# A linear-attention, mixture and gated-product kernel: whole-line values, denominators gathered in one transfer, conversions spread, weights split on another engine, and a re-planned order

## The chip, the core and the metric

The program runs on one NeuronCore of a Trainium2 chip. Its engines are TensorE (PE, whose weight loads the profile calls PEld), VectorE (DVE), ScalarE (ACT), GpSimd (POOL) and SyncE (SP), which here issues every transfer. The metric is the device time of one execution in microseconds (us); of several runs the median counts.

## What is computed

Three parts follow each other, all in fp32 (three of the late weights arrive as float64):

```python
def phi(x):
    proj = np.einsum('bhsd,df->bhsf', x, w_phi)
    proj = proj - np.max(np.abs(proj), axis=-1, keepdims=True)
    return np.concatenate([np.exp(proj), np.exp(-proj)], axis=-1)
q_p, k_p = (phi(q), phi(k))
kv = np.einsum('bhsf,bhsd->bhfd', k_p, v)
z = np.sum(k_p, axis=2)
num = np.einsum('bhsf,bhfd->bhsd', q_p, kv)
den = np.einsum('bhsf,bhf->bhs', q_p, z)[..., None] + 1e-06
x = num / den                                   # 4 x 8 heads, 576 tokens, 64 wide -> x: 2304 x 512
p = probs / (probs.sum(-1, keepdims=True) + 1e-09)
x = sum(p[:, e:e+1] * (np.maximum(x @ w1[e], 0) @ w2[e]) for e in range(4))   # 512 -> 1024 -> 512
out = ((x @ v1) * (x @ v2) @ w3) @ w_out        # 512 -> 1024 -> 1024 -> 512
```

## The kernel before

**Attention** goes by 16 pairs of heads. For pair p, `k_side` loads the keys (`kr`) and values (`vx`), projects the keys, subtracts the largest magnitude, takes both exponentials and sums them against the values (tile `kvp`, matmuls of line 498). The value tile holds, for each of five token tiles and two heads, 64 values and two columns of ones, which give the sum z; before the change the ones are set once by POOL and a load fills only the 64 columns. Pairs in `KSPLIT` do the key projection with each operand split into a rounded part and a remainder, three passes (`PASSES`); the others use one full-precision product. `q_side` does the same for the queries (`Pq`, `Ps`, `Eq`) and multiplies with `kvp`'s copy (`num`). The result `xq` has 64 rows of numerators and, in the other half, rows that all hold the denominator. One denominator row per head goes to DRAM (`den`), comes back as 128 partitions of 9 (`d9`, which the trace calls d), gets 1e-6 added and is inverted on DVE (lines 602, 605), goes to DRAM again (`rd`) and comes back broadcast over 64 partitions per head (`rb`); DVE multiplies (`xr`, line 615).

**Experts** go by visits: one visit is a quarter of one expert's hidden width, for one or two groups of 768 tokens. The first visits (`plain`) work on group 0 while attention is still running. Later visits use Strassen's seven products (`strassen_up`: banks upa, upb, upc; ACT copies a bank out as `s`, line 764; DVE adds them, line 771; `relu` makes the two parts of `h`; `expert_down` multiplies with w2, tile dn, and DVE adds to `acc`, line 833). Each weight is loaded as `raw` and split: ACT casts (line 290), then DVE or POOL subtracts (line 292); for Strassen POOL also forms sums (`sm`, line 326). Then come visits that `fold` w3 and w_out into one matrix (tile psw), taken in turn with experts, and last the gated products (`gates`), whose result `g` is split by ACT and DVE.

**Conversions.** The float64 weights become fp32 on the chip, in 40 half matrices (`nearest_tasks`, tile near): a load (line 342), one ACT step into a tile f (line 345), five DVE steps (lines 348, 351, 355, 358, 361), and a write-out of f to DRAM (line 364). There is one tile f, so the next ACT step waits for the write-out before it. `run_visits` puts these steps among the expert work. A visit's turn with one group starts a number of them: two in the turn of group 1, one in the other, 20 in the visits for groups 1 and 0, and 20 in those for groups 1 and 2.

**The order** on each engine is written out by a planner, `Prog.run`: it plays all operations with a duration for each (`ns`), a delay after a result (`TAIL`) and after a transfer (`wait`), and a priority, and emits them in the order in which they start there. `AHEAD` and `KLEAD` set the priority of each pair against the expert turns. Each engine then takes its list in order, and SyncE its transfers too.

The planner's delays and the pace of the conversions are in these lines:

```python
SYNC = 45.0
TAIL = {"PE": 175.0, "DVE": 85.0, "ACT": 100.0, "POOL": 85.0}
def dma(fn, nbytes, **kw):
    return op(SP, 500, fn, wait=1600 + nbytes / 180.0, **kw)
for _ in range(0 if len(pairs) < 2 else 1 + (i == 1)):
    if len(near_todo) > (20 if c >= KA else 0):
```

## Time and profile before

| what | value |
|---|---|
| median of 3 runs | 1337.9 us |
| lowest run | 1337.41 us |
| the profiled execution | 1336.39 us |
| its span, first to last instruction | 1334.6 us |
| mean granted PE clock | 0.991 of full speed |
| busy: PE, DVE, ACT, POOL | 1286.8, 972.0, 614.4, 478.3 us |

Busy is the time in which an engine's instructions run, in the profiled execution. A stretch of the span is read by itself: attention alone runs to 94 us, attention with plain visits to 338, the experts for groups 1 and 0 to 602, groups 1 and 2, then group 2, with the fold to 1052, and the gated products to the end. The waits name, for each idle time of an engine, whose signal ended it. The chain is the work that ended last, followed back from the end.

### The profile page before, as it was taken

To read this page: it belongs to the slowest core of one execution; us is meant where nothing else is said; L and a number is where in the kernel's file an instruction comes from. 1 tells how busy PE (TensorE), PEld (TensorE's weight loads), DVE (VectorE), ACT (ScalarE), POOL (GpSimd) and SP (SyncE) were. 2 spreads that over 40 slices of the span, in tenths; PEclk is the share of its full clock that TensorE was granted. 3 is DMA by queue.
4 is the path that set the end of the run, shared out by engine and by line. 5 is a ranking of instruction groups with operands and counts; after the bars stand their busy time and mean duration, and the time that the engine had idled before them with its cause. 6 is when DMAs were issued, how large, how long until landed. Compare 5 with 4: busy or idle time off the path is not lost.

```text
span 1334.6 us, 18054 instructions
## 1 busy us (share of the span) xinstructions
PE 1286.8 (96%) x6739; PEld 1154.1 (86%) x6739; DVE 972.0 (73%) x1513; ACT 614.4 (46%) x1198; POOL 478.3 (36%) x348
## 2 busy tenths in 40 slices
PE   8889999999999899999989999999999999999998
PEld 7778888998887788898878898988888899999897
DVE  6678898877977788877877888766656555476555
ACT  5677875763433233334333333443434454243451
POOL 3333321222432333302333333134465553244671
PEclk8999999999999999999999999999999999999999
DMA  5554443322333332203334333212232211013211
GB/s 146 147 167 110 136 134 114 90 66 58 103 104 102 103 103 95 87 32 111 127 110 151 126 127 111 78 58 80 103 111 97 85 32 34 30 33 110 80 48 48
DMA packets 73032, 126.28 MB, mean 95 GB/s; under 512 B 32720, under 2 KB 37200, under 8 KB 72944
## 3 DMA queue, kind: packets, MB, share of 16 engines
q1 hardware_dynamic: 72944, 125.13, 30.6%
q8 instruction: 53, 0.87, 0.3%
q14 instruction: 35, 0.29, 0.1%
HBM read 107.66 MB, written 17.45 MB: 94 GB/s over the span
## 4 chain that ended last, share of the span: by engine, by line
PE 62%; DVE 16%; DMA 11%; ACT 5%; issue 4%; POOL 1%; SPq 1%; ACTq 0%; POOLq 0%; DVEq 0%
PE dn L810 25%; PE upa L741 8%; PE upb L741 4%; PE kvp L498 3%; PE psw L883 2%; DMA rb<-rd 2%; DVE acc L833 2%; PE num L587 2%; DMA near_v<-near 2%; PE upc L741 2%; PE up L741 2%; DVE near L361 2%; DMA near_wo<-near 2%; DMA rd<-d 1%; PE upa_3b L741 1%
## 5 line engine op out<-in xcount | busy, mean ns | idle before, releaser
L810 PE MATMUL dn<-w_b,h 128*128 128x512 f32 x1728 | 424.9, 393 | 4.9 <-DVE acc L833 3.6
L810 PEld LDWEIGHTS dn<-w_b,h 128*128 128x128 f32 x1728 | 322.3, 189 | 66.5 <-DVE acc L833 5.2
L833 DVE SCALAR_TENSOR_TENSOR acc<-dn,pn,acc 128x512 f32<-128x512 f32 x270 | 198.3, 744 | 56.2 <-PE dn L810 55.3
L741 PE MATMUL upa<-x_T,w_a 128*128 128x384 f32 x720 | 148.7, 341 | 16.2 <-ACT s L764 16.1
L292 POOL TENSOR_TENSOR w_b<-raw_b,w_b 128x1024 fp32r<-128x1024 f32 x32 | 80.2, 2507 | 227.1 <-ACT w_b L290 227.1
L563 POOL PARTITION_ALL_REDUCE M<-Ps x64 | 86.3, 1352 | 200.1 <-ACT Ps L560 157.4
L741 PEld LDWEIGHTS upa<-x_T,w_a 128*128 128x128 f32 x720 | 127.7, 189 | 29.8 <-ACT s L764 24.7
L292 POOL TENSOR_TENSOR w_a<-raw_a,w_a 128x768 fp32r<-128x768 f32 x32 | 61.4, 1917 | 233.7 <-ACT w_a L290 233.6
L290 ACT CAST w_b<-raw_b 128x1024 fp32r<-128x1024 f32 x59 | 62.0, 1051 | 103.3 <-PE dn L810 64.9
L810 PE MATMUL dn<-w_b,g 128*128 128x512 f32 x432 | 104.5, 390 | 0.0
L764 ACT COPY s<-upa 128x384 f32<-128x384 f32 x120 | 57.3, 477 | 101.0 <-PE upa L741 100.7
L326 POOL TENSOR_TENSOR sm_a<-raw_a 128x256 f32<-128x256 f32 x64 | 52.5, 821 | 141.0 <-DMA raw_a<-w 60.6
L810 PEld LDWEIGHTS dn<-w_b,g 128*128 128x128 f32 x432 | 80.6, 188 | 14.2
L292 POOL TENSOR_TENSOR w_a<-sm_a,w_a 128x1024 fp32r<-128x1024 f32 x32 | 80.3, 2511 | 10.6 <-ACT w_a L290 10.6
L498 PEld LDWEIGHTS kvp<-vx,E 128*128 128x128 f32 x576 | 74.4, 202 | 6.4 <-ACT E L490 3.3
L587 PE MATMUL num<-Eq,KV 128*128 128x288 f32 x328 | 71.9, 348 | 6.9 <-ACT Eq L571 2.7
L498 PE MATMUL kvp<-vx,E 128*128 128x66 f32 (+1 forms) x576 | 75.9, 284 | 2.6 <-DMA vx<-vt 1.3
L741 PE MATMUL up<-x_B,w_a 128*128 128x384 f32 x384 | 71.7, 337 | 0.0
L741 PEld LDWEIGHTS up<-x_B,w_a 128*128 128x128 f32 x384 | 66.7, 188 | 0.6
L587 PEld LDWEIGHTS num<-Eq,KV 128*128 128x128 f32 x328 | 51.7, 191 | 15.8 <-ACT Eq L571 3.8
L290 ACT CAST w_a<-raw_a 128x768 fp32r<-128x768 f32 (+2 forms) x59 | 48.3, 818 | 35.7 <-PE upb L741 23.6
L571 ACT ACTIVATE Eq<-Ps 128x288 f32<-128x288 f32 x128 | 50.7, 444 | 22.0 <-DVE Ps L566 20.3
(217 smaller groups left out, 2416.2 us busy)
## 6 DMA issues: line engine op xcount, KB each, us to landing
raw_a<-w SPq DMA_DIRECT2D x35, 512.0 KB
raw_b<-w SPq DMA_DIRECT2D x35, 512.0 KB
qr<-qT SPq DMA_DIRECT2D x32, 288.0 KB
near<-w3T SPq DMA_DIRECT2D x16, 512.0 KB
raw_b<-near_wo SPq DMA_DIRECT2D x16, 512.0 KB
near<-v SPq DMA_DIRECT2D x16, 512.0 KB
vx<-vt SPq DMA_DIRECT2D x16, 320.0 KB
kr<-kT SPq DMA_DIRECT2D x15, 320.0 KB
```

The costliest lines, as they stand in the source:

```text
L290: lambda: op(ACT, act(n), lambda: nc.scalar.copy(out=hi(), in_=raw[1]()), reads=[raw[0]], fills=[w], after=after),
L292: lambda: op(eng, ns, lambda: e.tensor_tensor(out=lo(), in0=raw[1](), in1=hi().bitcast(F32), op=ALU.subtract), reads=[raw[0], w], fills=[w ...
L326: ops.append(lambda k=k, out_=out_, a=a, b=b, how=how: op(eng, ns, lambda: e.tensor_tensor(out=out_(), in0=a(), in1=b(), op=how), reads=[r ...
L361: lambda: op(DVE, dve(n), lambda: v.tensor_tensor(out=f(), in0=f(), in1=t(), op=ALU.add), reads=[t], writes=[f]),
L498: nc.tensor.matmul(kvp()[:, a].rearrange("p h d -> p (h d)") if rest else kvp()[:, a, h], E()[:, a] if rest else E()[:, t, a, h], w()[:, 4 ...
L563: op(POOL, 1171, lambda M=M, Ps=Ps: nc.gpsimd.partition_all_reduce(M(), Ps(), channels=128, reduce_op=bass_isa.ReduceOp.absmax), reads=[Ps ...
L571: op(ACT, act(HS), lambda a=a, E=E, Ps=Ps: nc.scalar.activation(out=E()[:, a], in_=Ps(), func=AF.Exp, scale=1.0 - 2 * a), reads=[Ps], fill ...
L587: nc.tensor.matmul(num(), KV[i]()[:, a, 2 * h:2 * h + 2].rearrange("p c d -> p (c d)"), EE[j]()[:, a], start=n == 0, stop=n == len(parts) - 1)
L741: nc.tensor.matmul(ps(), w()[:, a, i, kk * 128:kk * 128 + 128], x()[:, j, kk], start=first and n == 0, stop=last and n == total - 1, skip_ ...
L764: op(ACT, act(TB, False), lambda: nc.scalar.copy(out=t(), in_=ps()), reads=[ps], writes=[t], after=start["C"])
L810: nc.tensor.matmul(ps(), hs[fc]()[:, x, t * 128:(t + 1) * 128], w()[:, fc * 2:fc * 2 + 2, y], start=fc == 0 and n == 0, stop=fc == 1 and n ...
L833: op(DVE, dve(DM), lambda a=a, ps=ps, share=share: nc.vector.scalar_tensor_tensor(out=a(), in0=ps(), scalar=share(), in1=a(), op0=ALU.mult ...
```

## The change

- The host lays the values out with their columns of ones, so one load fills the whole tile; POOL's fills at the start are gone.
- The denominator row of each head goes straight from `xq` to 64 partitions of `d9`; the trip through `den` in DRAM is gone.
- Pair 13 leaves `KSPLIT`.
- Conversions: one per turn, 16 in the visits for groups 1 and 0, 16 for groups 1 and 2, and 8 in the visits for group 2 alone (`NEAR`, two in the first of these); v1 and v2 are taken by quarters.
- The fold's weights are split with POOL's subtraction in the 8 fold visits for quarters 0 to 7, DVE's after that.
- The gate product is written over its second operand, which lies in PSUM for three of four blocks, so that cast and subtraction read PSUM.
- The planner: 100 ns more after each result, 500 ns more after each transfer (`LATE`) and more for the small ones (`extra`), 6% on DVE and ACT (`MORE`), measured lengths for the conversion steps, other `KLEAD` and `AHEAD`.

```diff
-KSPLIT = (2, 4, 7, 10, 11, 12, 13, 14, 15)
+KSPLIT = (2, 4, 7, 10, 11, 12, 14, 15)
...
-AHEAD = (0.05, 0.53, 0.67, 0.83, 1.78, 1.99, 3.11, 3.51, 7.79, 8.19, 8.47, 9.88)
+AHEAD = (0.05, 0.53, 0.67, 0.83, 1.78, 1.99, 3.11, 4.01, 7.79, 7.93, 8.42, 9.83)
+NEAR = (24, 8, 0)
-BESIDE = 1.3
+BESIDE = 1.5
...
-        self.n, self.eng, self.ns, self.fn, self.prio, self.wait = n, eng, ns, fn, prio, wait
+        self.n, self.eng, self.fn, self.prio = n, eng, fn, prio
+        self.ns = ns * Prog.MORE if eng in ("DVE", "ACT") else ns
+        self.wait = wait + Prog.LATE if eng == "SP" else wait
...
-    TAIL = {"PE": 175.0, "DVE": 85.0, "ACT": 100.0, "POOL": 85.0}
+    TAIL = {"PE": 275.0, "DVE": 185.0, "ACT": 200.0, "POOL": 185.0}
+    LATE, MORE = 500.0, 1.06
...
-            out=w().rearrange("p t h d -> p (t h) d")[:, :, 0:64], in_=vt[b, pr].rearrange("p (c d) -> p c d", d=64)
-        ),
-            327680, writes=[w])
+        dma(lambda: nc.sync.dma_start(out=w().rearrange("p t h d -> p (t h d)"), in_=vt[b, pr]), 337920, writes=[w])
...
             dma(lambda h=h, dr=dr: nc.sync.dma_start(
-                out=den()[:, h * S:(h + 1) * S], in_=xq()[dr:dr + 1, h]
-            ), 2304, reads=[xq], fills=[den])
-        d9 = V("at", [128, 2 * S // 128], F32, "d9", 3, f"d9_{p}")
-        dma(lambda: nc.sync.dma_start(out=d9(), in_=den()[0].rearrange("(p c) -> p c", p=128)), 4608,
-            reads=[den], writes=[d9])
+                out=d9()[h * 64:(h + 1) * 64], in_=xq()[dr:dr + 1, h].rearrange("o (p c) -> o p c", p=64)
+            ), 2304, extra=1500, reads=[xq], fills=[d9])
...
-                lambda: n3().rearrange("p (k q f) -> p k q f", k=2, q=2)[:, :, q % 2], "ring1", f"a{v}", reads=[n3], n=2
+                lambda: n3().rearrange("p (k q f) -> p k q f", k=2, q=2)[:, :, q % 2], "ring1", f"a{v}", reads=[n3], n=2,
+                eng=POOL if c < KA else DVE
             ))
-            made.append(split_tasks(lambda: no(), "ring2", f"b{v}", reads=[no]))
+            made.append(split_tasks(lambda: no(), "ring2", f"b{v}", reads=[no], eng=POOL if c < KA else DVE))
...
-                    for _ in range(0 if len(pairs) < 2 else 1 + (i == 1)):
-                        if len(near_todo) > (20 if c >= KA else 0):
+                    phase = 2 if len(pairs) < 2 else int(c < KA)
+                    for _ in range(2 if phase == 2 and c == KA else 1):
+                        if len(near_todo) > NEAR[phase]:
...
-                        to = gates[ft]
-                        op(DVE, dve(TB), lambda to=to, src=src: nc.vector.tensor_tensor(
-                            out=to(), in0=src(), in1=to(), op=ALU.mult
-                        ), reads=[src], writes=[to])
+                        g = gates[ft]
+                        op(DVE, dve(TB), lambda g=g, src=src: nc.vector.tensor_tensor(
+                            out=src(), in0=src(), in1=g(), op=ALU.mult
+                        ), reads=[g], writes=[src])
...
-    for w in vx:
-        op(POOL, 1000, lambda w=w: nc.gpsimd.memset(w(), 1.0), writes=[w])
...
+    vpad = np.zeros((B, 4, 128, 5, 2, D + 2), v.dtype)
+    vpad[:, :, :, :4, :, D:] = 1
```

SyncE, while pairs 0 to 3 are under way (kr: keys, qr: queries, vx: values, the number behind each name is the pair). Before, from the gathering of pair 0's denominators to its broadcast:

```order
L596 DMA den0_332<-xq0_296 1x576
L534 DMA qr3_0_396<-qT 128x576
L600 DMA d9_0_415<-den0_332 128x9
L596 DMA den1_443<-xq1_406 1x576
L606 DMA rd0_453<-d9_0_415 128x9
L610 DMA rb0_479<-rd0_453 64x576 x2
```

and now:

```order
L600 DMA d9_0_359<-xq0_311 64x1x9
L600 DMA d9_1_463<-xq1_427 64x1x9
L607 DMA rd0_471<-d9_0_359 128x9
L538 DMA qr3_1_479<-qT 128x576
L443 DMA vx0_123<-vt 128x660
L600 DMA d9_1_463<-xq1_427 64x1x9
L611 DMA rb0_535<-rd0_471 64x576 x2
```

The first hop through DRAM is gone, and three other transfers have moved between rd0 and rb0.

ACT, in the visits for groups 1 and 0 (h12_0 and s12_0 are visit 12, group 0; near0 is the conversion's step into tile f). Before, between two conversion steps:

```order
L345 ACTIVATE near0_3831<-near0_3831 128x512
L290 CAST w_b13_4277<-raw_b13_4006 128x4x256
L796 ACTIVATE h12_0_00_4297<-upc12_0_4280 128x384
L764 COPY s2_12_0_4306<-upa12_0_4251 128x384
L764 COPY s3_12_0_4329<-upa12_0_4251 128x384
L796 ACTIVATE h12_0_11_4332<-s3_12_0_4329 128x384
L345 ACTIVATE near0_3831<-near0_3831 128x512
```

and now:

```order
L352 ACTIVATE near0_3799<-near0_3799 128x512
L297 CAST w_b13_4209<-raw_b13_3950 128x4x256
L766 COPY s1_12_0_4219<-upa12_0_4202 128x384
L766 COPY s2_12_0_4249<-upa12_0_4202 128x384
L798 ACTIVATE h12_0_00_4253<-upc12_0_4223 128x384
L766 COPY s3_12_0_4270<-upa12_0_4202 128x384
L798 ACTIVATE h12_0_11_4280<-s3_12_0_4270 128x384
L352 ACTIVATE near0_3799<-near0_3799 128x512
```

The next step stands seven places after the one before it, where it stood six, and group 0's turn now has one of them.

POOL, at visits 21 and 22 (w_a22 and w_b22: the expert's weights; w_a21 and w_b21: the fold's; sm: Strassen's sums). Before:

```order
L326 TENSOR_TENSOR sm_a22_6136<-raw_a22_6051,sm_a22_6136 128x256
L292 TENSOR_TENSOR w_a22_6292<-raw_a22_6051,w_a22_6292 128x3x256
L292 TENSOR_TENSOR w_a22_6292<-sm_a22_6136,w_a22_6292 128x4x256
L292 TENSOR_TENSOR w_b22_6366<-raw_b22_6060,w_b22_6366 128x4x256
L326 TENSOR_TENSOR sm_a24_6435<-raw_a24_6389 128x256
```

and now:

```order
L299 TENSOR_TENSOR w_a21_5950<-raw_a21_5828,w_a21_5950 128x2x256
L333 TENSOR_TENSOR sm_a22_6078<-raw_a22_5983 128x256
L333 TENSOR_TENSOR sm_a22_6078<-sm_a22_6078,raw_a22_5983 128x256
L333 TENSOR_TENSOR sm_a22_6078<-raw_a22_5983 128x256
L333 TENSOR_TENSOR sm_a22_6078<-raw_a22_5983,sm_a22_6078 128x256
L299 TENSOR_TENSOR w_b21_6138<-raw_b21_5902,w_b21_6138 128x4x256
L299 TENSOR_TENSOR w_a22_6206<-raw_a22_5983,w_a22_6206 128x3x256
L299 TENSOR_TENSOR w_a22_6206<-sm_a22_6078,w_a22_6206 128x4x256
L299 TENSOR_TENSOR w_b22_6280<-raw_b22_5994,w_b22_6280 128x4x256
```

The fold's two subtractions have come to stand among those of the expert after it.

## Rows read from the trace of the kernel before

**Rows 1.** Busy time by stretch: length, then busy us of each engine, PEclk, DMA

```profile
0.00:25.00 25.00, 21.64 (x93) 17.09 (x94) 15.37 (x34) 13.06 (x31) 8.31 (x17) 0.80 0.56 147
25.00:225.00 200.00, 185.64 (x1136) 165.60 (x1134) 161.19 (x301) 142.43 (x340) 59.67 (x45) 0.98 0.50 138
...
350.00:450.00 100.00, 91.76 (x436) 80.42 (x436) 80.37 (x118) 33.79 (x60) 41.68 (x30) 0.97 0.33 101
450.00:675.00 225.00, 220.89 (x1098) 196.16 (x1097) 181.96 (x275) 82.91 (x148) 60.41 (x38) 1.00 0.30 94
600.00:875.00 275.00, 266.96 (x1322) 237.05 (x1321) 221.64 (x332) 107.14 (x187) 78.00 (x52) 1.00 0.36 114
675.00:775.00 100.00, 93.07 (x456) 82.05 (x455) 77.01 (x120) 35.17 (x62) 26.08 (x20) 1.00 0.40 126
1075.00:1225.00 150.00, 150.00 (x786) 140.24 (x785) 82.19 (x125) 60.03 (x107) 64.75 (x49) 1.00 0.13 39
1225.00:1275.00 50.00, 48.03 (x246) 43.34 (x245) 32.08 (x47) 22.99 (x39) 29.53 (x23) 1.00 0.32 106
```

**Rows 2.** Waits, whole span: engine, line, releaser, us, times, longest

```profile
DVE xr L615 <- DMA rb<-rd: 16.7, 12, 4.2
PE upa L741 <- ACT s L764: 16.1, 17, 2.2
DVE d L602 <- DMA d<-den: 9.9, 7, 2.6
PE kvp L498 <- DMA vx<-vt: 1.3, 1, 1.3
```

**Rows 3.** Waits of SyncE's queue, whole span

```profile
SPq L600 <- DMA den<-xq: 18.8, 12, 4.8
```

**Rows 4.** Chain that ended last, 25 to 235 us: shares

```profile
by line: DMA rb<-rd 11.8%; DMA rd<-d 8.9%; PE kvp L498 7.3%; DVE xr L615 7.3%; PE num L587 6.2%; DMA d<-den 5.5%; issue 4.5%; DMA vx<-vt 4.4%; DMA den<-xq 3.9%; DVE Ps L566 3.0%; ACT Eq L571 2.9%; DVE w_a L292 2.2%; DMA raw_a<-w 2.1%; DVE E
```

**Rows 5.** Chain that ended last, 350 to 775 us: shares

```profile
by line: PE dn L810 23.6%; PE upa L741 12.6%; issue 6.7%; PE upb L741 5.7%; DMA near_v<-near 5.7%; DVE near L361 4.8%; DMA near_wo<-near 4.8%; DVE acc L833 4.5%; DMA near_w<-near 3.8%; DVE near L358 3.5%; DVE near L351 3.0%; DVE near L355 2
```

**Rows 6.** The conversion tile: ns min/median/max; last who waited for it

```profile
L355 DVE TENSOR_SCALAR near<-near x40: 409/418/2512, 355.5 to 838.8; 128x512 int32<-128x512 int32 x40
...
L361 DVE TENSOR_TENSOR near<-near x40: 674/684/2774, 358.3 to 841.8; 128x512 f32<-128x512 f32 x40
...
  ACT near L345: 50.4, 30
```

**Rows 7.** Chain pieces: key projections, full precision and split

```profile
20.75 0.86 PE P L463 x4
...
267.60 1.43 PE P L463 x12
```

**Rows 8.** Timeline 397 to 409 us: start, us, engine, instruction, idle before

```profile
397.73 2.17 DVE L351 SCALAR_TENSOR_TENSOR near<-near 128x512 int32<-128x512 int32 x1
...
399.30 2.86 POOL L292 TENSOR_TENSOR w_a<-sm_a,w_a 128x1024 fp32r<-128x1024 f32 x1
...
400.29 2.14 DVE L355 TENSOR_SCALAR near<-near 128x512 int32<-128x512 int32 x1
...
408.17 1.70 PE L741 MATMUL upa<-x_T,w_a 128*128 128x384 f32 x6 [2.23 <-ACT s L764]
```

**Rows 9.** Groups by shape: weight splits: count, busy us, mean ns

```profile
L292 POOL TENSOR_TENSOR w_b<-raw_b,w_b 128x1024 fp32r<-128x1024 f32 x32 | 80.2, 2507 | 227.1 <-ACT w_b L290 227.1
...
L292 DVE TENSOR_TENSOR w_b<-raw_b,w_b 128x1024 fp32r<-128x1024 f32 x27 | 37.0, 1371 | 3.3 <-ACT w_b L290 2.6 <-issue 0.4
L292 DVE TENSOR_TENSOR w_a<-raw_a,w_a 128x512 fp32r<-128x512 f32 x16 | 30.3, 1896 | 8.6 <-ACT w_a L290 8.6
```

**Rows 10.** The gate tile g: ns min/median/max

```profile
L292 DVE TENSOR_TENSOR g<-s_3a,g x12: 548/551/559, 1065.0 to 1201.7; 128x384 fp32r<-128x384 f32 x12
...
L292 DVE TENSOR_TENSOR g<-s_4a,g x12: 643/1653/2551, 1081.0 to 1226.3; 128x384 fp32r<-128x384 f32 x12
```

More of the change, by code (lines that the diff above doesn't have):

```diff
@@ L284, in beside, with split_ops @@
         return dve(n) * (BESIDE if "C" in start else 1)
-    def split_ops(raw, hi, lo, n, w, eng, after=()):
-        e, ns = (nc.gpsimd, gp(n)) if eng == POOL else (nc.vector, beside(n))
+    def split_ops(raw, hi, lo, n, w, eng, after=(), sbuf=True):
+        e, ns = (nc.gpsimd, gp(n)) if eng == POOL else (nc.vector, beside(n) if sbuf else dve(n))
         return [
-            lambda: op(ACT, act(n), lambda: nc.scalar.copy(out=hi(), in_=raw[1]()), reads=[raw[0]], fills=[w],
+            lambda: op(ACT, act(n, sbuf), lambda: nc.scalar.copy(out=hi(), in_=raw[1]()), reads=[raw[0]], fills=[w],
                        after=after),
@@ L504, in total @@
                             )
-            op(PE, 2 * mm4(132) if rest else nt * 4 * 210, total, reads=[E, w], writes=[kvp])
+            op(PE, 2 * mm4(132) if rest else nt * 4 * 224, total, reads=[E, w], writes=[kvp])
         for g, (t0, nt) in enumerate(KG0 if not p else KG):
@@ L797, in relu @@
            reads=[src], fills=[h])
-        op(DVE, dve(TB), lambda: nc.vector.scalar_tensor_tensor(
+        op(DVE, beside(TB) if sbuf else dve(TB), lambda: nc.vector.scalar_tensor_tensor(
             out=h()[:, 1], in0=src(), scalar=0.0, in1=h()[:, 0].bitcast(F32), op0=ALU.max, op1=ALU.subtract,
@@ L899, in run_visits @@
         turn, behind = 0, []
-        near_todo = deque((k, i, h) for k, n in (("wo", 4), ("w3", 8), ("v1", 4), ("v2", 4)) for i in range(n) for h in range(2))
+        near_todo = deque(
+            (k, i, h) for k, n in (("wo", range(4)), ("w3", range(8)), *((x, (c,)) for c in range(4) for x in ("v1", "v2")))
+            for i in n for h in range(2)
+        )
         srcs = {"wo": w_out, "w3": w3T, "v1": v1, "v2": v2}
@@ L903, in run_visits @@
         drain()
-        rooms, later = [None, None], []
+        rooms, later = {}, []
         for v, (kind, c, pairs, blocks) in enumerate(visits):
@@ L990, in fused_kernel @@
     qr0 = load_q(0, 0)
-    for w in vx:
-        op(POOL, 1000, lambda w=w: nc.gpsimd.memset(w(), 1.0), writes=[w])
-        for h in range(2):
-            op(POOL, 100, lambda w=w, h=h: nc.gpsimd.memset(w()[64 - 64 * h:128 - 64 * h, 4, h], 0.0), writes=[w])
     op(POOL, 1000, lambda: make_identity(nc, eye()), writes=[eye])
```

42 lines of the change are left out of this document (20 added, 22 removed).

## The prediction, on record before the kernel ran

> **What bounds the kernel now.** I read the busy time by stretch first, because the shares over the whole span hide that this program is two programs. TensorE (PE) is the engine everything else feeds: from 1075 to 1225 us it is busy 150.00 of 150 us, so nothing but its own work sets the time there [rows 1]. The question is therefore where PE is not full. Taking busy from length, PE is idle 3.36 us in the first 25 us, 14.36 in 25 to 225 (attention), 8.24 in 350 to 450, 4.11 in 450 to 675, 6.93 in 675 to 775 (expert work with conversions beside it), and 1.97 in 1225 to 1275 [rows 1]. These 39 us, and what a lower clock costs, are all that an order or a shorter wait can give back. The granted clock is 0.80 in the first 25 us, 0.98 in 25 to 225 and 0.97 in 350 to 450: 5, 4 and 3 us of PE time lost to stretches at 1.2 instead of 2.4 GHz [rows 1]. The two later ones lie in stretches that also have stalls.
>
> Then the waits, to see what the stalls end on. PE itself waits mostly for ScalarE's (ACT) copy of a bank (16.1 us, 17 times), hardly for a load: once, 1.3 us, for the values [rows 2]. VectorE (DVE) waits 16.7 us for the reciprocals that come back as rows (rb), and 9.9 us for the gathered denominators [rows 2]. SyncE's queue, in which all transfers stand in order, is held 18.8 us until the first of the two denominator transfers has landed [rows 3].
>
> Last the chain that ended last, in the stretches with losses. In 25 to 235 us the denominator's four transfers are on it: den 3.9%, d 5.5%, rd 8.9%, rb 11.8% of 210 us, and the values 4.4% [rows 4]. In 350 to 775 us the write-outs of converted weights are 14.3% of 425 us: 5.7 (near_v), 4.8 (near_wo), 3.8 (near_w) [rows 5]. ACT waits 50.4 us in 30 waits for these write-outs, since the next conversion's first step overwrites the tile that is still being written out [rows 6]. ACT takes its work in order, so the copies that free PE's banks stand behind that wait.
>
> **The change, part by part.**
>
> Denominators. Per pair, den and d (SBUF to DRAM, DRAM to SBUF) become one kind of transfer, SBUF row to 64 partitions. On the chain the two cost (3.9% + 5.5%) of 210 us = 19.7 us [rows 4]. One stays. Its price is in no row: from below it is nothing beyond the rest, from above it is the old pair of hops (64 pieces of 36 bytes where d had 128). I take half, so 10 us leave the chain, and SyncE's 18.8 us hold goes with the hop [rows 3]. In the new order of SyncE three other transfers stand between rd and rb, where before there was none (the order rows of the change), so the queue has work while rd lands. What is late next is rd and rb, which stay: 20.7% of 210 us [rows 4].
>
> Values. One run of 2,640 bytes a partition instead of ten of 256. The transfers on the chain are 4.4% of 210 = 9.2 us [rows 4]; I take a third off, 3 us, between 0 and all of it. At the start the memsets that the first one waited for also go; there PE waited 1.3 us for it [rows 2], so 1 us.
>
> These 13 us of chain are not 13 us of PE, because PE works on other pairs meanwhile. The cap is PE's 14.36 us of idle in this stretch [rows 1]. I take 8, with ends at 0 (the new order hides no more than the old) and 14.4. DVE is the cover that could fail: it is busy 161 of 200 us here [rows 1], so there is room to be earlier by 8 us, not by 40.
>
> Pair 13's keys. Three passes become one full-precision product. Two runs from the chain price it: 1.43 us for 12 records of the split kind, 0.86 for 4 of the other [rows 7]. The pair's 12 split records become 8: 1.43 against 1.72 us. With the small last tile it is nothing either way, and one cast and one subtraction leave ACT and DVE. Cost 0.
>
> Conversions spread. 40 half matrices, 20 and 20 in two stages, become 16, 16 and 8, one a turn. Each stage to 775 us thus carries a fifth less, and in ACT's queue the steps stand 7 rows apart where they stood 6 (order rows). PE's idle there is 8.24 + 4.11 + 6.93 = 19.3 us [rows 1]. A fifth of it is 3.9 us, if losses go with the number; all of it, if the write-outs never hold ACT again. I take 9, nearly the middle. The clock: the fall in 400 to 410 us stands behind a PE wait of 2.23 us [rows 8]; I let 3 of the 7 us lost to the clock from 25 us on go with the stalls. The third stage, after 875 us, gets 8 conversions of five DVE steps of 0.42 to 0.68 us [rows 6], 2.9 us each; PE's load there is unchanged and DVE has room. 0.
>
> Fold weights on GpSimd (POOL). 16 subtractions leave DVE: 8 at 1.371 and 8 at 1.896 = 26 us of its 221.64 busy us in 600 to 875 [rows 1, 9]. POOL gains 8 at 2.507, and 8 of half as many columns, an estimate of half of that, 1.25: together 30 us on top of 78 in 275 [rows 1, 9]. Nothing waits for them unless they come late, a whole visit ahead. I take 0, between -3 (DVE's relief reaches PE) and the second rival.
>
> Gate products stay in PSUM. DVE's subtraction after a gate takes 1.653 us at the median in one block and 0.551 in another, with the same shape [rows 10], so up to 1.1 us each is waiting. But PE is full there [rows 1]; the cover makes it free. Of the 1.97 us idle in 1225 to 1275 I take 0 to 2: 0. A price is that PSUM banks are held through cast and subtraction, 0.55 us for the subtraction [rows 10] and the cast before it; I count 0, and at worst the stretch's 1.97 us once more.
>
> A rule of the Trainium skill bears on the last two parts (page "SBUF — State Buffer", section "SBUF: two separate sides"): DVE instructions with two SBUF inputs, or in a fast two-port mode, and GpSimd instructions take one port pair by exclusive lock, and the loser blocks for the whole instruction. The trace agrees: a 0.42 us conversion step took 2.14 us beside a POOL subtraction of 2.86 us [rows 6, 8]. The rule favours the gate part and speaks against the fold part; what it would make of the sum is the second rival.
>
> Sum: 8 + 1 + 9 + 3 = 21 us. The profiled execution took 1336.4 us (span 1334.6 and 1.8 around it); it becomes 1315.4. The median of the runs is 1.5 us above it, so 1316.9: I forecast 1317.
>
> **The rivals.**
>
> First, attention gives nothing, since DVE and the two transfers that stay bound it, and the conversions give only their fifth: 1 + 4 + 1 (clock) = 6 us, 1332. For it: rd and rb cost the chain twice what is saved [rows 4], and DVE is 81% busy [rows 1]. Against it: PE idles in 25 to 225 us at all, and DVE's waits of 9.9 us end on exactly the transfer that is cut [rows 2].
>
> Second, the slower side: POOL's 16 new subtractions in 600 to 875 us block DVE steps that PE waits for. Two blocked steps of 2.17 and 2.14 us in a row ended in a PE wait of 2.23 us [rows 8]. Should each of the 16 do that, 35 us are added: 1317 + 35 = 1352. It decides the sign from 21/16 = 1.3 us of PE wait for each. For it: POOL's 768- and 1024-column subtractions already do this. Against it: the subtractions that leave DVE were themselves blocked (1.896 us for half the columns that took 1.371) [rows 9], so blocking moves more than it grows.
>
> Third, all waits go: 14.4 + 19.3 + 7 (clock) + 1 at the start = 41.7 us, 1296. For it: one cause (an in-order queue behind a transfer) stands behind both stretches. Against it: ACT's bank copies also stand behind POOL's lock, which stays [rows 8].
>
> Fourth, the spreading doesn't do what it says: the order rows show 7 instead of 6 places between steps, hardly a turn. Then 9 and 3 fall away and 1329 is left; it goes with the first.
>
> **How the numbers follow.** My forecast, 1306 to 1326, has 0.47; the first and fourth together 0.25; the third, down to 1296, 0.18; the second 0.10. The range leaves out little at either end: 1299 to 1338. Two per cent, 26.8 us, is about what a measurement of this kernel can tell from no change. Faster by more means under 1311: the third and about a third of the forecast's band, 0.33. Slower by more needs over 1364, beyond even 1352 of the second: 0.04. Within: 0.63.
>
> **What would show it.** Right: PE idle in 25 to 225 us near 6 us, and in 350 to 775 near 10; ACT's wait for write-outs under 30 us; DVE's wait for d9 under 5 us; no half-clock stretch at 400 to 450. The forecast is wrong on attention if DVE's waits for rb grow by what those for d9 lose. It is wrong on the fold if conversion steps over 2 us become more frequent in 600 to 875 us and PE's waits for ACT or DVE with them.

## The result and the profile after

| | median us | runs | against before, on the same chip |
|---|---|---|---|
| before | 1337.66 | 4 | |
| changed kernel | 1305.13 | 4 (1304.2 to 1306.09) | 0.976, 95% interval 0.9741 to 0.9779 |

The changed kernel is faster by 2.4%, 32.5 us. Two single runs, 1565.86 us of before here and 1797.48 us of the kernel with the new pace alone further down, stand far from the others of their kernels and have no part in any ratio. The time lies in the forecast's range (1299 to 1338), 12 us below the forecast of 1317 and beyond the 2% that it held likeliest.

Profiled, the changed kernel took 1304.2 us, of which the span is 1302.0. Here are the first part of its page (busy time and instructions of each engine) and the chain of the whole span by engine:

```profile
PE 1273.9 (98%) x6734; PEld 1154.0 (89%) x6734; DVE 940.8 (72%) x1496; ACT 611.6 (47%) x1197; POOL 505.2 (39%) x358
...
PE 87%; DVE 7%; ACT 3%; issue 1%; DMA 1%; SPq 0%; POOL 0%; ACTq 0%; DVEq 0%
```

The busy time by stretch, for the stretches of [rows 1], without that from 600 to 875 us, and for two more; the columns are the same:

```profile
0.00:25.00 25.00, 21.97 (x105) 17.39 (x105) 15.76 (x37) 13.39 (x32) 5.92 (x10) 0.86 0.56 171
25.00:225.00 200.00, 194.50 (x1245) 178.45 (x1245) 180.79 (x327) 156.59 (x375) 67.34 (x49) 1.00 0.48 145
350.00:450.00 100.00, 99.12 (x495) 89.16 (x494) 80.89 (x125) 35.63 (x64) 38.08 (x27) 1.00 0.31 101
450.00:675.00 225.00, 224.71 (x1126) 202.19 (x1125) 164.17 (x258) 85.66 (x152) 75.86 (x47) 1.00 0.27 88
675.00:775.00 100.00, 100.00 (x495) 89.65 (x494) 75.64 (x119) 35.95 (x64) 41.82 (x27) 1.00 0.39 124
775.00:925.00 150.00, 145.72 (x722) 128.71 (x721) 113.44 (x157) 65.06 (x111) 61.81 (x42) 1.00 0.34 116
925.00:1075.00 150.00, 145.75 (x745) 131.72 (x744) 90.66 (x127) 70.06 (x121) 75.41 (x56) 1.00 0.22 76
1075.00:1225.00 150.00, 144.10 (x732) 133.58 (x731) 80.13 (x132) 52.71 (x91) 61.68 (x47) 0.97 0.17 60
1225.00:1275.00 50.00, 50.00 (x265) 47.17 (x264) 20.19 (x35) 24.40 (x41) 36.33 (x28) 1.00 0.13 43
```

Read length less PE's busy time, as the forecast did. From 25 to 225 us the idle time falls from 14.36 to 5.5 us, and PE fits 1245 matmuls where it had 1136. From 350 to 775 it falls from 19.3 to 1.2, and the stretch at 1.2 GHz behind a stall at 409 us is gone: the clock there is 1.00. But the two lines from 775 to 1075 show 4.28 and 4.25 us idle, and from 1075 to 1225, where before was full [rows 1], 5.9 us are idle and the clock is 0.97. So this change gives something back late in the program, where the forecast had put 0.

The waits, of the whole span, with the column order of [rows 2]; no line for DVE and rb or d is left in the list:

```profile
PE num L591 <- ACT xq L596: 4.0, 6, 0.9
PE upa L743 <- ACT s L766: 0.3, 1, 0.3
PE kvp L502 <- DMA vx<-vt: 0.4, 1, 0.4
```

From 25 to 225 us alone, the longest waits of PE were these before:

```profile
PE Pq L555 <- ACT Ps L560: 5.1, 7, 2.0
PE num L587 <- ACT Eq L571: 2.7, 2, 1.5
```

Now the 4.0 us for xq above are the longest there, and those for Ps are gone. In neither kernel does a wait of PE in this stretch end on a transfer of the denominators or on DVE's product with rb.

The conversion tile, to be held against [rows 6]; the last line is the wait of ACT for the write-outs:

```profile
L355 DVE TENSOR_SCALAR near<-near x40: 406/419/1993, 335.3 to 950.0; 128x512 int32<-128x512 int32 x40
...
L368 DVE TENSOR_TENSOR near<-near x40: 674/682/2774, 341.9 to 953.3; 128x512 f32<-128x512 f32 x40
...
  ACT near L352: 19.6, 13
```

PE's wait for ACT's bank copies went from 16.1 us to 0.3, the wait of ACT for write-outs from 50.4 us in 30 waits to 19.6 in 13. The chain from 350 to 775 us, by line, no longer has a transfer among its larger shares, where [rows 5] had 14.3% of them:

```profile
by line: PE dn L812 48.6%; PE upa L743 24.2%; PE upb L743 12.3%; PE upc L743 5.7%; PE psw L885 4.5%; DVE near L368 1.0%; issue 0.8%; PE tr L846 0.6%; DVE upc L773 0.4%; ACT h L798 0.3%; DVE near L365 0.3%; DVE x_B L299 0.3%; ACT w_b L297 0.
```

**Where the time came from.** Idle time is not all that PE loses: a matmul that starts late by less than its own length still counts as busy, and so does one at half clock. I therefore went through the trace and added up, for each pair of matmuls that follow each other, the time between their starts less what such a pair takes when nothing holds it (0.227 us for 512 columns, 0.1745 for 384, 0.11 to 0.24 for attention's). That lost time is 87.5 us before and 54.3 after. The difference, 33.2 us, is the whole gain of the span (1334.6 - 1302.0 = 32.6), while idle time fell only from 47.8 to 28.1 (span less busy). By stretch, with the experiments that follow (one profiled execution each; us):

| kernel | 0-25 | 25-225 | 225-350 | 350-775 | 775-1075 | 1075-end | sum |
|---|---|---|---|---|---|---|---|
| before | 9.2 | 30.9 | 4.9 | 31.3 | 6.7 | 4.6 | 87.5 |
| changed | 8.1 | 14.4 | 1.2 | 5.1 | 13.9 | 11.7 | 54.3 |
| before with margins alone | 9.3 | 28.4 | 0.9 | 13.4 | 6.1 | 11.5 | 69.6 |
| changed without margins | 9.7 | 28.8 | 3.0 | 12.9 | 21.5 | 5.2 | 81.0 |
| before with the new pace alone | 10.6 | 36.3 | 5.4 | 9.5 | 7.6 | 4.5 | 73.8 |
| changed with the old pace | 8.5 | 14.2 | 1.2 | 11.3 | 13.1 | 11.7 | 60.0 |
| changed, no margin on results (late only) | 9.8 | 28.5 | 3.3 | 8.6 | 14.9 | 5.1 | 70.1 |
| changed, no margin on transfers | 10.1 | 19.4 | 1.0 | 10.1 | 13.1 | 11.5 | 65.2 |
| changed, denominators through DRAM | 6.2 | 25.0 | 1.6 | 6.5 | 13.5 | 11.3 | 64.2 |
| changed, values in pieces | 7.7 | 20.8 | 1.1 | 7.2 | 16.5 | 11.4 | 64.7 |
| changed, old priorities | 6.2 | 19.3 | 3.1 | 7.1 | 15.6 | 11.4 | 62.8 |
| changed, fold split on DVE | 9.2 | 14.2 | 1.3 | 8.2 | 15.8 | 11.2 | 60.0 |
| changed, gate product in SBUF | 4.9 | 14.2 | 1.6 | 8.1 | 14.1 | 11.9 | 54.8 |
| changed, no margins in the gated products | 5.2 | 14.1 | 1.6 | 4.7 | 11.5 | 4.9 | 42.0 |

The change wins 16.5 + 3.7 us in attention, 26.2 with the conversions and 1.1 at the start, and pays 7.2 and 7.1 in the last two stretches. One execution differs from the next by some us in this table, so small differences are left to the ratios: the run with the gate product in SBUF has the changed kernel's list of PE instructions up to 1025 us and loses 8.1 where that one loses 5.1. What an undisturbed pair takes is a choice in attention: with the median of each shape the column from 25 to 225 us is 14 to 17 us higher in every row, and differences between rows change by up to 3; from 350 us on nothing changes by more than 0.6.

### The profile page after: what moved, and what is told of

Same layout as the page of the kernel before. It is cut to its first block, busy times and chain, and to the rows that moved or that the text cites. A ratio compares the mean times of both kernels' runs of the same rounds, so it can differ in the third digit from the quotient of the medians.

```text
span 1302.0 us, 17975 instructions
## 1 busy us (share of the span) xinstructions
PE 1273.9 (98%) x6734; PEld 1154.0 (89%) x6734; DVE 940.8 (72%) x1496; ACT 611.6 (47%) x1197; POOL 505.2 (39%) x358
## 4 chain that ended last, share of the span: by engine, by line
PE 87%; DVE 7%; ACT 3%; issue 1%; DMA 1%; SPq 0%; POOL 0%; ACTq 0%; DVEq 0%
PE dn L812 36%; PE upa L743 12%; PE upb L743 6%; PE up L743 4%; PE kvp L502 3%; PE psw L885 3%; PE upc L743 3%; PE num L591 3%; PE upa_5a L743 1%; PE P L467 1%; PE upa_3a L743 1%; PE upa_3b L743 1%; PE upa_4b L743 1%; PE upa_4a L743 1%; PE upa_5b L743 1%
## 5 line engine op out<-in xcount | busy, mean ns | idle before, releaser
L299 POOL TENSOR_TENSOR w_b<-raw_b,w_b 128x1024 fp32r<-128x1024 f32 x40 | 99.9, 2499 | 264.1 <-ACT w_b L297 256.1
L299 POOL TENSOR_TENSOR w_a<-raw_a,w_a 128x768 fp32r<-128x768 f32 (+1 forms) x40 | 71.8, 1794 | 198.6 <-ACT w_a L297 198.6
L812 PEld LDWEIGHTS dn<-w_b,g 128*128 128x128 f32 x432 | 80.7, 188 | 14.2
L502 PEld LDWEIGHTS kvp<-vx,E 128*128 128x128 f32 x576 | 71.7, 196 | 2.8 <-DMA vx<-vt 0.8
L502 PE MATMUL kvp<-vx,E 128*128 128x66 f32 (+1 forms) x576 | 72.7, 277 | 1.0 <-PE P L467 0.5
L591 PEld LDWEIGHTS num<-Eq,KV 128*128 128x128 f32 x328 | 51.1, 189 | 11.9 <-ACT xq L596 5.7
```

The lines of the kernel that those rows point to most:

```text
L299: lambda: op(eng, ns, lambda: e.tensor_tensor(out=lo(), in0=raw[1](), in1=hi().bitcast(F32), op=ALU.subtract), reads=[raw[0], w], fills=[w ...
L502: nc.tensor.matmul(kvp()[:, a].rearrange("p h d -> p (h d)") if rest else kvp()[:, a, h], E()[:, a] if rest else E()[:, t, a, h], w()[:, 4 ...
L591: nc.tensor.matmul(num(), KV[i]()[:, a, 2 * h:2 * h + 2].rearrange("p c d -> p (c d)"), EE[j]()[:, a], start=n == 0, stop=n == len(parts) - 1)
L812: nc.tensor.matmul(ps(), hs[fc]()[:, x, t * 128:(t + 1) * 128], w()[:, fc * 2:fc * 2 + 2, y], start=fc == 0 and n == 0, stop=fc == 1 and n ...
```

## The experiments

Every edit is planned anew, so each run is an edit and the order that the planner makes of it. All were timed in three rounds beside before on the same chip; ratios are against before, and the changed kernel's own is 0.976.

**The planner's margins.** The forecast had no term for `TAIL`, `LATE` and `MORE`. First they are given to the kernel before, with nothing else of the change:

```diff
-    TAIL = {"PE": 175.0, "DVE": 85.0, "ACT": 100.0, "POOL": 85.0}
+    TAIL = {"PE": 275.0, "DVE": 185.0, "ACT": 200.0, "POOL": 185.0}
+    LATE, MORE = 500.0, 1.06
```

> The kernel before with nothing changed but the planner's margins: 100 ns more after each result, 500 ns more after each transfer, 6% on VectorE and ScalarE. Theory A (the gain comes from the shorter denominator route and the rarer conversions, as forecast): the margins alone give at most 5 us, so 1333 us or more. Theory B (the gain comes from the order, which no longer puts an instruction where its transfer is only just due): most of the 32.5 us is there already, 1306 to 1320 us, with TensorE's idle in 350 to 775 us under 8 us though the conversions come as densely as before.

Measured: 1320.68 against 1340.77 us, 0.9853 (0.9818 to 0.9887), at the slow edge of B's band, with PE idle for 7.6 us from 350 to 775. Then the change without them; the longer delays of the small transfers (`extra`) and the new lengths of the planner's operations stay:

```diff
-    TAIL = {"PE": 275.0, "DVE": 185.0, "ACT": 200.0, "POOL": 185.0}
+    TAIL = {"PE": 175.0, "DVE": 85.0, "ACT": 100.0, "POOL": 85.0}
-    LATE, MORE = 500.0, 1.06
+    LATE, MORE = 0.0, 1.0
```

> The changed kernel with the planner's margins back as before (results 100 ns earlier, transfers 500 ns earlier, no 6%), all else as changed. Theory A: 1305 to 1312 us, since the shorter route and the pace stay. Theory B: 1320 us or more, with ScalarE's waits for the write-outs and VectorE's for transfers back over 60 us in sum.

Measured: 1331.19 against 1340.77, 0.9927 (0.9912 to 0.9943). So the margins are worth 1.5% on the old kernel and 1.7% on the new, and all other parts together 0.7% without them. The lines below, of the change without margins, are its waits of DVE for rb and d over the whole span, ACT's wait for the write-outs, and the busy time in attention and beside the conversions:

```profile
DVE xr L616 <- DMA rb<-rd: 2.9, 4, 1.8
...
DVE d L603 <- DMA d<-xq: 1.9, 1, 1.9
```

```profile
  ACT near L352: 12.2, 13
```

```profile
25.00:225.00 200.00, 185.90 (x1152) 166.83 (x1151) 166.74 (x304) 146.82 (x347) 61.34 (x46) 0.98 0.47 139
...
350.00:775.00 425.00, 419.34 (x2078) 373.36 (x2076) 325.49 (x496) 155.37 (x275) 159.61 (x106) 1.00 0.31 101
```

The time came as B said, the waits did not: 4.8 and 12.2 us, 17 in sum, where B wanted over 60. DVE's waits for the two transfers fell from 26.6 us [rows 2] to 4.8, and yet PE has 14.1 us idle from 25 to 225, as in [rows 1], and loses 28.8 there instead of 30.9. These waits stood in the waits and in the chain, and taking them away gave attention next to nothing by itself. The margins alone gave it as little (28.4). Only together do the losses fall to 14.4.

Nor did the route of the denominators become shorter in time. By the trace, in medians over the 16 pairs, the second broadcast is issued 15.1 us after the first gathering transfer before, 15.0 us in this kernel and 15.1 in the changed one. What moved is DVE: it uses d 4.1 and 4.6 us after the issue of the last gathering transfer, where it was 2.9 before, and rb 3.7 and 4.6 us after the issue of its second half, where it was 2.3. The planner's `extra` asks for just that, and it is in force in this kernel too. So these waits went in good part because the order puts DVE's instructions later.

Which margin it is, the next two split. One keeps those on results and drops the one on transfers:

```diff
-    LATE, MORE = 500.0, 1.06
+    LATE, MORE = 0.0, 1.06
```

> The changed kernel without the 500 ns on transfers; the 100 ns on results and the 6% stay. If spare time on transfers is what the margins give: 1320 us or more, the loss before 600 us. If spare time on results is: 1302 to 1309 us. Were both needed, it stands between.

Measured: 1316.57 against 1339.82, 0.9837 (0.9811 to 0.9863). The other keeps the one on transfers and drops the 100 ns on results and the 6%:

```diff
-    TAIL = {"PE": 275.0, "DVE": 185.0, "ACT": 200.0, "POOL": 185.0}
+    TAIL = {"PE": 175.0, "DVE": 85.0, "ACT": 100.0, "POOL": 85.0}
-    LATE, MORE = 500.0, 1.06
+    LATE, MORE = 500.0, 1.0
```

> The changed kernel with the 500 ns on transfers alone; results as before and no 6%. If spare time on transfers is what counts: 1303 to 1310 us. If spare time on results counts: 1322 us or more, and the gated products, which hold few transfers, go back from 289 to 282 us because the lengthening of that stage comes from the spare time on results.

Measured: 1319.06 against 1339.82, 0.9848 (0.9826 to 0.9869). Both stand about halfway (0.9927 without either, 0.976 with both), so both are needed, as the first expectation allowed; the time of the second lies between its two bands. The table places them: the margin on results, with the 6% that this run does not separate from it, brings attention from 28.5 to 14.4 and costs 6.6 after 1075 us; dropping the one on transfers costs 5.0 both in attention and beside the conversions.

**The pace of the conversions.** Undone in the changed kernel, then made alone in the kernel before (the same edit, the other way round):

```diff
-                    phase = 2 if len(pairs) < 2 else int(c < KA)
-                    for _ in range(2 if phase == 2 and c == KA else 1):
-                        if len(near_todo) > NEAR[phase]:
+                    for _ in range(0 if len(pairs) < 2 else 1 + (i == 1)):
+                        if len(near_todo) > (20 if c >= KA else 0):
```

> The changed kernel with the conversions at the old pace (20 and 20, two in one turn and one in the next), margins kept. Theory A: the conversions' share comes back, 12 us by the forecast's terms, so about 1317 us. Theory B: 1305 to 1309 us, because the margins keep the steps apart from the write-outs at either pace; the third stage, from 850 us on, loses its 8 conversions and gains up to 3 us.

Measured: 1309.02 against 1340.77, 0.9761 (0.9746 to 0.9776): nothing is lost that the ratios can tell, to about 3 us.

> The kernel before with only the conversions' new pace (one per turn; 16, 16 and 8). The two remedies for ScalarE's wait for write-outs, the pace and the margins, seem to stand in for each other: without margins at the new pace the stretch from the last plain projection to the fold took 252.5 us, with margins at the old pace 250.5, before 268.3. If so, this kernel's stretch is 252 to 258 us and the total 1322 to 1330 us by before's 1338. If the pace does nothing by itself: 1336 us or more.

Measured: 1321.07 against 1339.82, 0.9853 (0.9826 to 0.988): as much as the margins alone. The stretch from the last plain projection to the fold takes 253.5 us, as expected. Below are its line of waits and its busy time, then the same of the changed kernel at the old pace:

```profile
  ACT near L347: 35.8, 23
```

```profile
350.00:775.00 425.00, 420.98 (x2094) 376.72 (x2094) 329.96 (x514) 158.61 (x281) 127.95 (x89) 1.00 0.31 99
```

```profile
  ACT near L352: 8.2, 12
```

```profile
350.00:775.00 425.00, 419.46 (x2085) 375.62 (x2084) 341.97 (x517) 159.06 (x282) 152.47 (x99) 1.00 0.34 109
```

Pace and margins are two cures for one stall. Either alone brings PE's idle time there from 19.3 us to 4 to 8 (4.0 with the pace, 7.6 with margins alone, 5.5 with margins and the other parts at the old pace). Both bring it to 1.2; the profiled executions still show 6.2 us of lost time between the change with the old pace and with the new (11.3 and 5.1), of which the ratio shows nothing. The sum of ACT's waits is no measure of it: with the new pace alone it falls by 15 us only, from 50.4 to 35.8, and most of the stall is gone; with the old pace and margins it is 8.2, less than the 19.6 of the full change, and no time is gained by that.

What the stalls of the kernel before stand behind tells more. One of them, after the DVE steps of [rows 8]:

```profile
407.25 0.49 ACT L796 ACTIVATE h<-upc 128x384 fp32r<-128x384 f32 x1 [6.15 <-DVE upc L771]
407.64 0.47 ACT L764 COPY s<-upa 128x384 f32<-128x384 f32 x1
```

PE waits for this copy until 408.17 us, the copy stands behind h in ACT's list, and h has waited 6.15 us for DVE, not for a write-out. Read so, one by one, 8.8 of the 19.3 us (8 stalls) stand behind such an h, with 4 to 5 us of conversion steps in DVE's 8 us before it; 3.6 us (4 stalls) end on DVE's acc; only 5.6 us (5 stalls) stand behind an ACT step that waited for a write-out. By this reading the conversions hold PE up mostly through DVE's list, and the pace relieves that too: with it alone 2.5 us are left behind h and 0.3 behind write-outs.

**The parts of attention.** The denominators again through DRAM:

```diff
-                out=d9()[h * 64:(h + 1) * 64], in_=xq()[dr:dr + 1, h].rearrange("o (p c) -> o p c", p=64)
-            ), 2304, extra=1500, reads=[xq], fills=[d9])
+                out=den()[:, h * S:(h + 1) * S], in_=xq()[dr:dr + 1, h]
+            ), 2304, reads=[xq], fills=[den])
+        d9 = V("at", [128, 2 * S // 128], F32, "d9", 3, f"d9_{p}")
+        dma(lambda: nc.sync.dma_start(out=d9(), in_=den()[0].rearrange("(p c) -> p c", p=128)), 4608,
+            reads=[den], writes=[d9])
```

> The changed kernel with the denominators going through DRAM again (two transfers in place of one), margins kept. Theory A: 8 us come back, about 1313 us, all before 340 us of the span. Theory B: 1305 to 1308 us: the longer route is planned for, and the chain still has room.

Measured: 1310.7 against 1340.77, 0.977 (0.9734 to 0.9806). By the ratio the second trip is worth 0.1%, and by its interval between nothing and 0.5% (6 us); the time lies between the two bands. Its one profiled execution loses 10.6 us more from 25 to 225 us than the changed kernel's, but has two stretches at the 1.2 GHz level there, 13.6 us long together, where the changed kernel's has none, and its four runs reach from 1305.17 to 1315.33 us. So what the shorter trip gives under the margins stays open between nothing and 6 us. DVE's waits for rb stay gone in this run, and those for d are 4.2 us, where before had 9.9: they do not hang on the shorter trip alone. That trip by itself, on the kernel before, was not run. The values in pieces of 256 bytes, with POOL's fills:

```diff
-        dma(lambda: nc.sync.dma_start(out=w().rearrange("p t h d -> p (t h d)"), in_=vt[b, pr]), 337920, writes=[w])
+        dma(lambda: nc.sync.dma_start(
+            out=w().rearrange("p t h d -> p (t h) d")[:, :, 0:64], in_=vt[b, pr].rearrange("p (c d) -> p c d", d=64)
+        ),
+            327680, writes=[w])
```

> The changed kernel with the values loaded in ten pieces of 256 bytes a partition again and the ones set by GpSimd at the start. By the forecast's terms 1 us at the start and about 2 of attention's 8 come back: 1307 to 1309 us. If the whole lines are worth nothing by themselves because the margins cover the load: 1304 to 1307 us. If they carry attention's 21 us: 1312 us or more.

Measured: 1313.5 against 1339.82, 0.9815 (0.9792 to 0.9838): the values are worth 0.55%, about 7 us, the largest of these parts; in the table it is 6.4 us in attention. The time is in the last band, but of attention's 20 us only these come back. And the old priorities:

```diff
-KLEAD = (0, -10, -20, -10, 60, 20, 0, 20, 40, -10, 0, 40, 60, 20, -20, 0)
+KLEAD = (0, -10, 20, 20, 60, 20, 0, 20, 40, 0, 0, 40, 60, 20, 10, 0)
-AHEAD = (0.05, 0.53, 0.67, 0.83, 1.78, 1.99, 3.11, 4.01, 7.79, 7.93, 8.42, 9.83)
+AHEAD = (0.05, 0.53, 0.67, 0.83, 1.78, 1.99, 3.11, 3.51, 7.79, 8.19, 8.47, 9.88)
```

> The changed kernel with the old tables of priorities (KLEAD and AHEAD), all else as changed. Attention with its plain visits shrank by 21 us (334 to 313 us at the last plain projection), and neither the margins alone (328) nor the parts without margins (331) gave that. Theory B1 (margins and the shorter transfers together fill attention; the tables only shift pairs): within 3 us of the changed kernel, 1303 to 1309 us. Theory B2 (the tables bring the pairs 6 to 11 forward, and that is what fills attention): 1313 us or more, the last plain projection at 322 us or later.

Measured: 1312.57 against 1341.78, 0.9807 (0.9759 to 0.9855). The interval reaches 0.976, so these numbers are worth something between nothing and 1%. The time lies between the two bands, and the last plain projection ends at 315.9 us, far from B2's 322. Whether the difference is the priorities' merit, or what any new order may cost, stays open.

**The fold's weights and the gate products.** The subtractions back to DVE:

```diff
-                lambda: n3().rearrange("p (k q f) -> p k q f", k=2, q=2)[:, :, q % 2], "ring1", f"a{v}", reads=[n3], n=2,
-                eng=POOL if c < KA else DVE
+                lambda: n3().rearrange("p (k q f) -> p k q f", k=2, q=2)[:, :, q % 2], "ring1", f"a{v}", reads=[n3], n=2
             ))
-            made.append(split_tasks(lambda: no(), "ring2", f"b{v}", reads=[no], eng=POOL if c < KA else DVE))
+            made.append(split_tasks(lambda: no(), "ring2", f"b{v}", reads=[no]))
```

> The changed kernel with the fold's 16 subtractions on VectorE again. If their move is worth nothing by itself (forecast): 1303 to 1308 us. If VectorE's relief reaches TensorE: 1309 to 1315 us, lost between 565 and 880 us. If GpSimd's subtractions held VectorE up (the rival on the slower side): under 1302 us, with fewer conversion steps over 2 us in that stretch.

Measured: 1308.5 against 1341.78, 0.9761 (0.971 to 0.9812). The stretch from 565 to 875 us with the subtractions on DVE, then in the changed kernel, and a conversion step there (count, busy us, mean ns) in the same order:

```profile
565.00:875.00 310.00, 307.14 (x1529) 273.68 (x1528) 240.54 (x356) 124.39 (x217) 96.45 (x66) 1.00 0.32 108
```

```profile
L362 DVE TENSOR_SCALAR near<-near 128x512 int32<-128x512 int32 x18 | 8.6, 480 | 0.1
```

```profile
565.00:875.00 310.00, 308.54 (x1543) 276.37 (x1542) 227.45 (x344) 125.15 (x219) 122.84 (x80) 1.00 0.34 111
```

```profile
L362 DVE TENSOR_SCALAR near<-near 128x512 int32<-128x512 int32 x19 | 12.8, 672 | 0.2
```

POOL takes 26.4 us more, DVE is relieved of 13.1 only, and the conversion step grows from 480 to 672 ns at the mean. That is the blocking which the second rival feared; but PE's idle time there is 1.5 us against 2.9, so nothing of it reaches PE there. Of the conversion steps in this stretch 4 take over 2 us in the changed kernel and 1 with the subtractions on DVE, as the third theory said, but no time comes with it. The gate product back in SBUF:

```diff
-                        g = gates[ft]
-                        op(DVE, dve(TB), lambda g=g, src=src: nc.vector.tensor_tensor(
-                            out=src(), in0=src(), in1=g(), op=ALU.mult
-                        ), reads=[g], writes=[src])
+                        to = gates[ft]
+                        op(DVE, dve(TB), lambda to=to, src=src: nc.vector.tensor_tensor(
+                            out=to(), in0=src(), in1=to(), op=ALU.mult
+                        ), reads=[src], writes=[to])
```

> The changed kernel with the gate product written to SBUF as before. The last stage became 8 us longer with the change (281 to 289 us), and it did so too with the margins alone (288.6), not without them (282.5). So the gate product should not be the cause: 288 to 290 us for that stage and 1303 to 1308 us in all. If holding PSUM through cast and subtraction had cost it: stage under 284 us, total under 1301 us.

Measured: 1305.27 against 1341.78, 0.9745 (0.9703 to 0.9787). No difference can be told, and the loss after 1075 us is there as well (11.9 us). It isn't PSUM that the gated products lack.

**What the gated products lose.** The timeline of the changed kernel where they stall (start, us, engine, instruction, idle before):

```profile
1200.45 1.22 PE L743 MATMUL upa_5a<-x_T,w_a 128*128 128x384 f32 x6
1200.78 0.96 DVE L299 TENSOR_TENSOR x_T<-xsum,x_T 128x768 fp32r<-128x768 f32 x1 [0.90 <-ACT x_T L297]
...
1203.07 1.04 ACT L297 CAST w_b<-raw_b 128x1024 fp32r<-128x1024 f32 x1 [0.88 <-PE dn L812]
1203.07 0.69 DVE L865 TENSOR_TENSOR oacc<-dn,oacc 128x512 f32<-128x512 f32 x1 [1.32 <-PE dn L812]
1203.67 0.95 DVE L673 TENSOR_TENSOR xsum<-xr 128x768 f32<-128x768 f32 x1
...
1204.19 2.64 POOL L299 TENSOR_TENSOR w_b<-raw_b,w_b 128x1024 fp32r<-128x1024 f32 x1 [15.14 <-ACT w_b L297]
...
1204.66 0.83 ACT L297 CAST x_T<-xsum 128x768 fp32r<-128x768 f32 x1 [0.55 <-DVE xsum L673]
1205.52 2.12 DVE L299 TENSOR_TENSOR x_T<-xsum,x_T 128x768 fp32r<-128x768 f32 x1 [0.90 <-ACT x_T L297]
...
1205.54 0.69 PE L743 MATMUL upa_5a<-x_T,w_a 128*128 128x384 f32 x1 [2.51 <-ACT x_T L297]
...
1207.70 1.97 PE L743 MATMUL upa_5a<-x_T,w_a 128*128 128x384 f32 x5 [1.47 <-DVE x_T L299]
```

DVE makes a sum (xsum), ACT casts it, DVE subtracts, and PE needs both. DVE's list has an addition to the output (oacc) before the sum, and that waits 1.32 us for PE; so the sum starts at 1203.67 us only, and PE stands 2.51 us. ACT's cast of w_b comes just before, so that POOL's subtraction of w_b falls beside DVE's of x_T, which takes 2.12 us (0.96 us for the one before it), and PE stands 1.47 more. From 1205.0 us on, within the first of these waits, the granted clock is at the 1.2 GHz level for 10.2 us: matmuls of 384 columns follow each other at 320 ns there, at 177 ns at 1200. Without its waits PE loses 4 us in that stretch. Stall (3.98) and clock together are 8 us, and the stage grows by 8 (280.9 to 289.0 us, from the first gate product to PE's end). Every kernel of the table with the margin on results (and the 6%) in this stage loses 11 to 12 us after 1075, every one without them about 5. In a stage where PE was already full [rows 1] the margin has nothing to win, and the order it makes is worse. So the last experiment leaves them out for the operations of these visits alone:

```diff
-        self.ns = ns * Prog.MORE if eng in ("DVE", "ACT") else ns
-        self.wait = wait + Prog.LATE if eng == "SP" else wait
+        self.ns = ns * Prog.MORE if eng in ("DVE", "ACT") and not Prog.tight else ns
+        self.wait = wait + Prog.LATE if eng == "SP" and not Prog.tight else wait
+        self.tail = Prog.TAIL.get(eng, 0.0) - (100.0 if Prog.tight and eng in Prog.TAIL else 0.0)
...
+            Prog.tight = kind == "gates"
```

> The changed kernel with the margins left out for the operations of the gated products alone (results, transfers and lengths there as the planner had them before). If the margins' order is what lengthens the last stage: that stage 281 to 284 us instead of 289, no half-clock stretch at 1205 us, total 1296 to 1300 us. If the stage is longer for another reason (the work now finds its inputs later): 1303 to 1308 us.

Measured: 1294.0 against 1341.78 us (1291.84 to 1300.01), 0.9666 (0.9617 to 0.9714): faster than both kernels, by 0.9 points over the change. Its waits of PE from 1005 to 1300 us, and the busy time around the stall's place:

```profile
PE upa_5b L747 <- ACT s_5b L770: 1.1, 2, 0.6
PE dn L816 <- DVE g L303: 0.8, 1, 0.8
PE upa_5a L747 <- ACT s_5a L770: 0.6, 1, 0.6
PE upa_4b L747 <- DVE g L303: 0.2, 1, 0.2
```

```profile
1075.00:1225.00 150.00, 147.47 (x764) 136.38 (x763) 83.35 (x134) 57.82 (x100) 67.75 (x53) 1.00 0.18 61
```

At the place of the stall the sum now stands before the addition to the output, and the cast of w_b after both (at 1197.66 us):

```profile
1192.66 0.96 DVE L677 TENSOR_TENSOR xsum<-xr 128x768 f32<-128x768 f32 x1
...
1194.94 0.69 DVE L869 TENSOR_TENSOR oacc<-dn,oacc 128x512 f32<-128x512 f32 x1 [1.32 <-PE dn L816]
1195.55 0.95 DVE L303 TENSOR_TENSOR x_T<-xsum,x_T 128x768 fp32r<-128x768 f32 x1
```

PE's list is the changed kernel's up to 1016 us, so this is the margins' effect in that stage. The waits for x_T are gone, the clock stays at 1.00, and the stage takes 282.6 us again; the time is 2 us below the expected band. In the profiled execution 6.4 of the 12 us come from here; another 3 come from the first 25 us, where this execution ran at full clock and the changed kernel's did not.

## Why the prediction was right, and where it was off

Direction and range held; the size was 21 us forecast against 32.5 measured, and a result within 2% had been called likeliest. That the range held is in part luck: without the margins, which the sum did not price, everything else in the change gives 0.7%, some 10 us, half of the 21.

- **Margins of the planner: the step that failed.** The list of the change names them, and the sum has no term for them, nor for `extra`, the new lengths and the tables of priorities. Alone the margins are worth 1.5% of 1340.77, 20 us. The forecast asked of each wait which transfer ended it, and not how close to its operand the order puts each instruction.
- **Denominators, forecast 8 (10 us off the chain).** The waits moved as told: DVE's for d are gone, and those for rb too, though rd and rb stay. But the route did not lose the time: up to the second broadcast's issue it takes 15.1 us a pair as before, and DVE's instructions stand later in the order. And the time did not follow from the waits: with all the edits but no margins attention loses 28.8 us where it lost 30.9. Under the margins the shorter trip is worth 0.1% by the ratio, 6 us at most by its interval. What the runs showed in place of the step is 20 us in attention (30.9 + 4.9 to 14.4 + 1.2), of edits and margins together. The cap of 14.36 us was also too low: that was idle time, and the loss was 30.9.
- **Values, forecast 3 of 13 on the chain and 1 at the start.** Undone, they cost 0.55%, 7 us. The mechanism isn't separated from the order that came with it.
- **Conversions 9 and clock 3.** Right that the pace pays, too small (the middle of 3.9 and 19.3, which the 9 is called near to, is 11.6), and the wait was only in part the one named: a write-out stands behind 5.6 of the 19.3 us of idle time, DVE's list behind 12.4. 26 us of lost time went from 350 to 775 us, of which the pace alone takes 22 (31.3 to 9.5). The third rival's "all waits go" came true in this stretch. But the pace is not needed: undone, it costs nothing that the ratios can tell, because the margins do most of the same work. The fourth rival, that spreading does not do what it says, falls by the pace alone.
- **Fold 0, gate products 0.** Both right as edits, to the 0.5% or so that their intervals leave. The second rival falls for the fold's subtractions: DVE's steps were blocked, but steps over 2 us did not become more frequent from 600 to 875 us (5 before, 3 now), and PE didn't wait for them. What the forecast missed at the end is again the margins' doing: 7 us from 1075 on, beside a further 7 from 775 to 1075. The cause of the latter stays open: the edits without margins lose more there (21.5), the margins or the pace alone on the kernel before do not (6.1 and 7.6), and undoing the pace, the fold or the gate products one at a time leaves it (13.1, 15.8, 14.1). The planner's new lengths, which no run undoes, are in all of these. The trace of the changed kernel shows what the two longest stalls there end on, 4.6 of 8.5 us of idle time. The longer one:

```profile
997.67 2.36 POOL L299 TENSOR_TENSOR w_b<-raw_b,w_b 128x1024 fp32r<-128x1024 f32 x1
997.83 2.62 DVE L800 SCALAR_TENSOR_TENSOR h<-s,h 128x384 fp32r<-128x384 f32 x1
...
1000.97 1.42 PE L812 MATMUL dn<-w_b,h 128*128 128x512 f32 x5 [2.49 <-DVE h L800]
```

This DVE step takes 0.56 us at 880.88. The other, 2.14 us at 885.11, stands behind a conversion step of the third stage (2.11 us at 882.29, 0.69 at the median) beside a POOL subtraction of 1.82 us. So the blocking of the second rival does reach PE, though not by the subtractions that were moved: both stalls are there with those back on DVE too. "DVE has room" did not cover the third stage's 8 conversions, though leaving them out, with the old pace, gives next to nothing back in that stretch (13.1 against 13.9).

- **Pair 13's keys 0.** Not tried by itself.
- **What was to show it.** PE idle from 25 to 225 us near 6: 5.5. Near 10 from 350 to 775: 1.2. Write-out waits under 30 us: 19.6. Waits for d under 5: none. No half clock at 400 to 450: none. All came true, the second by far more than forecast; but the idle time in attention and the waits did so for reasons other than those given, which only the experiments could tell. That 5.5 stands so near 6 is luck: the forecast had no term for the margins, without which 14.1 are left.

## What to carry to other kernels

When an order is planned ahead, spare time in the plan is a term of its own: price it before any transfer, and give it only where the critical engine has slack to spend, since in a full stage the same margin cost 7 us, about half of it by a stretch at half clock. A wait that stands in the list and on the chain isn't time until its removal, by itself, shortens the stage; it can also vanish because the planner puts the waiting instruction later. Two remedies for one stall must not be added. And look at lost time between starts, not only at idle time: here the busy share hid nearly half of it.
